# A planned attention, MoE and soft-MoE kernel on one core: new planner costs, w_in scaled by column block, a fourth scale part, the last g on VectorE, Exp loaded behind the last Mish

## The chip, the cores and the metric

The kernel runs on one core of one Trainium2 chip. The metric is device time in microseconds: the median of several executions, and lower is better. The engines are named as the profile names them: PE is TensorE (PEld its weight loads), ACT is ScalarE, DVE is VectorE, POOL is GpSimd, and SP issues the transfers.

## The reference

Three layers follow each other. The first is attention with a causal window of 64 keys, over 4 batches, 8 heads, 576 positions and head size 64. Its output is a matrix x of 2304 tokens by 512. The second is a dense layer pair with the Mish function between. The third is a soft mixture of experts with 32 slots.

```python
x = softmax(mask(q @ k.T / 8)) @ v              # per head; then 2304 x 512
h = x @ w_in                                    # 512 -> 2048
g = h * tanh(softplus(h))                       # Mish
x = g @ w_out                                   # 2048 -> 512
logits = x @ phi                                # 512 -> 32 slots
d = softmax(logits, axis=0);  slot_in = d.T @ x
slot_out[e] = relu(slot_in[e] @ w1[e]) @ w2[e]  # 8 experts, 4 slots each
out = softmax(logits, axis=1) @ slot_out
```

## The kernel before

The 2304 tokens are cut into 18 tiles of 128. **Attention** of a tile t has these operations, named by their planner names: qk (scores s, PE), max and neg (DVE), exp (ACT), sum and rcp (DVE), nrm (normalisation of p, POOL), tr (transposes pt on PE), tre (copies pts, ACT), pv (px on PE) and x (copy of the result). **The first dense layer** splits x and w_in into a high and a low half-precision part (xh and xl; wh and wl), so that each 128x512 block of h takes 12 matmuls; the planner cuts them into two halves, mm{t}_{m}a and mm{t}_{m}b, for the four column blocks m = 0 to 3 of w_in. ACT applies Mish (mi), and g is split again into gh and gl (gg in the profile). **w_out is never multiplied token by token**: the weights of w_out and phi are joined first (wpmm; wt are the tiles of the transposed w_out), so logits (lg) come from g directly, and the sum over tokens d.T @ g is kept up to date block by block of one or two tiles (bm, bexp, A, Aup). g is transposed by DMA (gT), for the last tile by PE (pghT, pglT). **The tail** multiplies that sum with w_out (si), then runs the experts: w1 (eh) and w2 (eo, by column blocks W2C), and last the outputs (fo, ob, out).

Weights arrive as 64-bit numbers and are decoded: a load of 512 KB (wir, wtr, wor), one ACT operation (wiy, wty, woy; L274) and two on DVE (L279, L283). Expert weights w are loaded as they are: 64 loads of 512 KB.

What sets the order of the work: a planner (class Plan) that runs when the program is built. Each operation has an engine, a cost in microseconds, a due time, operations that it depends on, and buffers that it takes and gives back (49 slabs of SBUF, 8 banks of PSUM, and counts that limit a kind). The planner steps through time; whenever an engine is free it issues the ready operation with the lowest due time whose buffers are free. Costs and due times are numbers in the dictionary PRM and in the calls of op. SAME and INTO are delays that it adds between operations. The result is a fixed order for each engine, and the same order for the DMA issues on SP's queue.

When PE has nothing to do in three stretches (from the start to qk0, from there to mm0_3a, and from the last h to t1_0), the planner issues a filler matmul there, 128x256 (fill, L194; pad in the profile). Fillers are instructions like others: once in the order, PE runs them whether it would have waited or not.

ACT holds one function table at a time. Exp and the decoding operation share one ("E"), Mish has the other ("M"), and copies run with either. Where the order changes from one to the other, an ACT_TABLE_LOAD stands between.

Scales: x and v are scaled by powers of two that come from running maxima of v over parts of the tiles (PART: three parts, tiles 0 to 3, 4 to 9 and 10 to 17). The chain that makes a scale is scale_ops (tr, mx, bc, f1 to f4).

Of the kernel before, what the change touches and what calls it, by code (L numbers as in the profile page):

```python
# [8 lines left out]
F32 = mybir.dt.float32  # L9
# [25 lines left out]
class Plan:  # L35


    SAME = {"DVE": 0.13, "ACT": 0.09, "PE": 0.0, "POOL": 0.0, "SP": 0.0, "NONE": 0.0}
    INTO = {"DVE": 0.2, "ACT": 0.2, "PE": 0.16, "POOL": 0.2, "SP": 0.1, "NONE": 0.0}
    DMA = 2.2  # L40
    SWITCH = 1.3
# [39 lines left out]
    def give(self, o):  # L81
        for key in o[7]:
            self.refs[key] -= 1
            if not self.refs[key]:
                p, i = self.where[key]
                q = p.rstrip("!^")
                self.free[q].append(i)
                if p != q:
                    self.held[p] -= 1

    def emit(self):
# [16 lines left out]
        while events:  # L108
# [6 lines left out]
            for eng in list(ready):  # L115
# [44 lines left out]
def body(tc, a):  # L160
# [7 lines left out]
    with ctx:  # L168
# [38 lines left out]
        sc = fix.tile([128, 56], F32, name="sc")  # L207
# [3 lines left out]
        SX, IX, SP_, IP, IL, C30, C31, CP, WM, SW, IW, INVH, GW, GV, GP_, RAT = 0, 3, 6, 7, 8, 11, 14, 17, 20, 24, 28, 32, 44, 48, 51, 52  # L211
        PART = [0 if t < 4 else 1 if t < 10 else 2 for t in range(NT)]
# [46 lines left out]
        def decode_ops(nm, src, n, where, dst, t_ld, t_dec, ld_deps, dst_get, y_eng):  # L259
# [25 lines left out]
            for j in range(n):  # L285
# [132 lines left out]
        for t in range(NT):  # L418
# [3 lines left out]
            for c in [1, 0] if 2 * t % 9 == 8 else [1]:  # L422
                one, end = t in (0, 4, 10) and c == 1, t in (3, 9, 17)
# [5 lines left out]
            for h in range(2):  # L429
                e = k + 2.6 * h  # L430
                op(f"max{t}_{h}", "DVE", 0.7, e + 1.5, lambda t=t, h=h: t_max(t, h), [f"qk{t}"] + ([f"max{t}_0"] if h else []))
                op(f"neg{t}_{h}", "DVE", 0.1, e + 1.5, lambda t=t, h=h: t_neg(t, h), [f"max{t}_{h}"])
                op(f"exp{t}_{h}", "ACT", 2.35 if t < P["SUMA"] else 1.5, e + 2, lambda t=t, h=h: t_exp(t, h), [f"neg{t}_{h}"] + ([f"exp{t}_0"] if h else []),
                   get=[] if h else [(f"p{t}", "s!"), (f"P{t}", "pp")], rel=[f"s{t}_{h}", f"S{t}_{h}"], table="E")
                if t >= P["SUMA"]:
                    op(f"sum{t}_{h}", "DVE", 0.7, e + 3, lambda t=t, h=h: t_sum(t, h), [f"exp{t}_{h}"] + (["sum%d_0" % t] if h else []))
                if h:
                    op(f"rcp{t}", "DVE", 0.25, e + 4, lambda t=t: t_rcp(t), [f"sum{t}_1" if t >= P["SUMA"] else f"exp{t}_1"])
                op(f"nrm{t}_{h}", *(("POOL", 1.3) if t < P["NRM"] else ("DVE", 0.72)), e + 4.5, lambda t=t, h=h: t_norm(t, h), [f"rcp{t}"] + ([f"nrm{t}_0"] if h else []))
                op(f"tr{t}_{h}a", "PE", 0.55, e + 5.5, lambda t=t, h=h: a_tr(t, h), [f"nrm{t}_{h}", "cst"], get=[(f"pt{t}_{h}", "b")], rel=[f"p{t}", f"P{t}"])  # L440
                op(f"tre{t}_{h}", "ACT", 0.62, e + 5, lambda t=t, h=h: t_trev(t, h), [f"tr{t}_{h}a"] + ([f"tre{t}_0"] if h else []),
# [3 lines left out]
            op(f"x{t}", *(("ACT", 0.62) if t < P["XA"] else ("DVE", 0.7)), k + 9, lambda t=t: t_x(t), [f"pv{t}"] + ([f"x{t - 1}"] if t % 2 else []),  # L445
# [4 lines left out]
        decode_ops("wi", a["w_in"], 16, lambda j: (j % 4, j // 4), stg, lambda j: P["W0"] + P["W_SP"] * j,  # L450
                   lambda j: P["W_DEC"] * (j + 1), [], "s", "POOL")
# [51 lines left out]
        for i, t in enumerate((3, 9, 17)):  # L503
# [56 lines left out]
        op("wpev", "DVE", 0.6, tw, wphi_ev, ["wpmm3"], get=[("wps", "s")], rel=["wpo"])  # L560
# [3 lines left out]
        for i in range(3):  # L564
            op(f"wpil{i}", "DVE", 0.15, tw if i == 0 else ta((3, 9, 17)[i]) - P["LEAD"] + 10, lambda i=i: wphi_il(i), ["p_f3", f"invc{i}"])
        op("wph", "ACT", 0.6, tw, wphi_h, ["p_s", "wptr"])
# [66 lines left out]
        for t in range(NT):  # L633
            t0 = T2 + TT * t
            last = [f"x{t // 2}"]
            op(f"xh{t}", "DVE", 0.54, t0 - 5, lambda t=t: x_h(t), [f"v{PART[t]}_s", f"x{t}"] + ([f"xh{t - 1}"] if t else []), get=[] if t % 2 else [(f"xx{t // 2}", "s!"), (f"XX{t // 2}", "x2")], rel=last)
            op(f"xl{t}", "DVE", 0.8, t0 - 4, lambda t=t: x_l(t), [f"xh{t}"], rel=last)
            for m in range(4):
# [5 lines left out]
                op(f"mi{t}_{m}", "ACT", 0.69, k + 2.7, lambda t=t, m=m: u_mish(t, m), [f"invh{PART[t]}_{0 if PART[t] else m}", f"mm{t}_{m}b"] + ([f"mi{t}_{m - 1}"] if m % 2 else []),  # L644
                   get=[] if m % 2 else [(f"u{t}_{h}", "s!"), (f"U{t}_{h}", "u")], rel=[f"h{t}_{m}"], table="M")
            U = units(t)
            for i, (h, c, n) in enumerate(U):
# [31 lines left out]
        op("idh", "DVE", 0.1, 60, id_half, ["cst"])  # L679

# [100 lines left out]
        for b in range(NBLK):  # L781
# [10 lines left out]
            op(f"lr{b}", "DVE", 0.3 + 0.07 * n, e, lambda b=b: b_lr(b), [f"lg{b}_{n - 1}_1", f"wpil{PART[t]}"], rel=[f"lg{b}"])  # L792
# [401 lines left out]
```

## Time and profile before

| what | value |
|---|---|
| median of 3 runs | 397.94 us (397.88 to 398.8) |
| profiled execution: time | 398.63 us |
| its span, first to last instruction | 396.8 us |
| mean granted clock of TensorE in the span | 0.986 |
| PE, ACT, DVE, POOL busy | 97%, 69%, 68%, 24% |
| moved by DMA | 102.67 MB, 259 GB/s |

The span is 1.8 us below the profiled execution's time, and that execution is 0.7 us above the median. The stages by the clock of the trace: the first scores at 6.4 us, the first block of h at 46.3 us, the last px at 224.5 us, the last block of h ends at 324.6 us, the experts begin at 344 us, the span ends at 396.8 us.

### The profile page before, as it was taken

What the parts mean: (1) busy time and instruction counts of PE and PEld (TensorE: products, weight loads), DVE (VectorE), ACT (ScalarE), POOL (GpSimd) and SP (SyncE); (2) the same over time, 40 slices, a digit from 0 to 9 for tenths busy, and PEclk for the clock granted to TensorE, in tenths of its full rate; (3) what the DMA queues carried; (4) which work ended last, traced back from release to release, by engine and by line L of the source; (5) the groups of instructions that cost most, each with busy time, mean ns of one, the idle gap of its engine ahead of it and who ended that gap; (6) DMA issues with size and microseconds to landing.
All of it is one profiled execution on the core that took longest, in us unless ns stands there. A gap on an engine that the chain in (4) does not pass through costs nothing.

```text
span 396.8 us, 10326 instructions
## 1 busy us (share of the span) xinstructions
PE 383.6 (97%) x4245; PEld 227.2 (57%) x4245; DVE 268.6 (68%) x579; ACT 275.8 (69%) x461; POOL 97.2 (24%) x82
## 2 busy tenths in 40 slices
PE   8999999999999999999999999999999999998982
PEld 6887758555465565566455644444454457636552
DVE  1799888879998969669899977455343374342342
ACT  1677799799986899878898399999655653102131
POOL 0243420205762222247140412121211240100000
PEclk9999999999999999999999999999999999999986
DMA  7999997131599784368999899999998889699997
GB/s 266 403 411 405 393 378 266 59 123 40 101 233 279 276 283 161 116 157 213 219 162 217 173 275 252 292 283 261 265 220 244 244 247 367 249 412 408 405 358 232
DMA packets 100686, 102.67 MB, mean 259 GB/s; under 512 B 74016, under 2 KB 81312, under 8 KB 100640
## 3 DMA queue, kind: packets, MB, share of 16 engines
q1 hardware_dynamic: 100640, 102.02, 85.9%
q8 instruction: 33, 0.54, 0.5%
q14 instruction: 13, 0.11, 0.1%
HBM read 79.46 MB, written 4.72 MB: 212 GB/s over the span
## 4 chain that ended last, share of the span: by engine, by line
PE 89%; DMA 4%; DVE 3%; issue 2%; ACT 0%; SPq 0%; DVEq 0%
PE h L587 47%; PE pad L194 6%; PE px L398 5%; PE pt L385 4%; PE eo L924 4%; PE eh L892 3%; PE s L332 3%; PE A L766 3%; DMA v<-in_vL 3%; PE lg L690 2%; PE lg L692 2%; PE fo L977 1%; DMA q<-in_qL 1%; PE gram_v L374 1%; PE s L323 1%
## 5 line engine op out<-in xcount | busy, mean ns | idle before, releaser
L587 PE MATMUL h<-wh,xx 128*128 128x512 f16 x576 | 184.3, 379 | 0.0
L587 PEld LDWEIGHTS <-xx 128*128 128x128 f16 x864 | 80.4, 98 | 86.4 <-issue 1.8
L587 PE MATMUL h<-wl,xx 128*128 128x512 f16 x288 | 109.1, 379 | 0.0
L364 POOL TENSOR_TENSOR p<-p,st 128x512 f32<-128x512 f32 x36 | 45.7, 1289 | 121.9 <-DVE st L344 34.1
L607 POOL TENSOR_SCALAR gg<-u,sc 128x1024 f16<-128x1024 f32 (+1 forms) x38 | 47.7, 1261 | 108.8 <-ACT u L593 86.1
L593 ACT ACTIVATE u<-h,sc 128x512 f32<-128x512 f32 x72 | 48.4, 686 | 28.0 <-PE h L587 23.4
L612 DVE SCALAR_TENSOR_TENSOR gg<-u,sc,gg 128x1024 f16<-128x1024 f32 (+1 forms) x38 | 50.3, 1332 | 13.8 <-POOL gg L607 13.8
L593 ACT ACT_TABLE_LOAD x41 | 52.6, 1283 | 2.0 <-PE h L587 1.3
L350 ACT ACTIVATE p<-s,st 128x128 f32<-128x128 f32 x144 | 41.8, 377 | 2.8 <-DVE st L344 2.5
L194 PE MATMUL pad<-wphi 128*64 128x256 f16 x259 | 36.5, 290 | 0.9 <-DVE wphi L204 0.9
L194 PEld LDWEIGHTS <-wphi 128*64 128x64 f16 x259 | 27.7, 116 | 5.5 <-issue 2.1
L390 ACT COPY pts<-pt 128x512 f32<-128x512 f32 x36 | 20.9, 588 | 11.4 <-PE pt L385 8.3
L341 DVE TENSOR_REDUCE st<-s 128x4 f32<-128x512 f32 x36 | 24.6, 683 | 5.4 <-PE s L332 5.4
L274 ACT ACT_TABLE_LOAD x19 | 24.4, 1283 | 1.0 <-PEq L1187 0.7
L356 DVE TENSOR_REDUCE st<-p 128x4 f32<-128x512 f32 x34 | 22.9, 674 | 2.4 <-ACT p L350 2.4
L385 PE MATMUL pt<-cst,p 128*128 128x128 f32 x144 | 21.6, 278 | 0.0
L398 PE MATMUL px<-pts,v 128*64 128x64 f32 x576 | 21.4, 225 | 0.0
L398 PEld LDWEIGHTS px<-pts,v 128*64 128x64 f32 x576 | 18.9, 138 | 3.7 <-issue 3.1
L332 PE MATMUL s<-k,q 64*64 64x128 f32 x576 | 18.8, 269 | 0.4 <-DMA q<-in_qL 0.4
L385 PEld LDWEIGHTS pt<-cst,p 128*128 128x128 f32 x144 | 16.1, 141 | 5.3 <-issue 3.0
L332 PEld LDWEIGHTS s<-k,q 64*64 64x64 f32 x576 | 16.9, 133 | 1.9 <-issue 0.7
L924 PE MATMUL eo<-w,hT 128*32 128x128 f32 (+1 forms) x384 | 16.9, 317 | 1.0 <-issue 1.0
(175 smaller groups left out, 491.8 us busy)
## 6 DMA issues: line engine op xcount, KB each, us to landing
w<-in_wL SPq DMA_DIRECT2D x64, 512.0 KB, 6.6
v<-in_vL SPq DMA_DIRECT2D x18, 512.0 KB, 8.3
wir<-in_w_in SPq DMA_DIRECT2D x16, 512.0 KB, 9.7
wtr<-in_w_outT SPq DMA_DIRECT2D x16, 512.0 KB, 4.9
wor<-in_w_out SPq DMA_DIRECT2D x16, 512.0 KB, 5.2
k<-in_kL SPq DMA_DIRECT2D x12, 512.0 KB, 8.8
q<-in_qL SPq DMA_DIRECT2D x9, 512.0 KB, 10.2
out<-ob SPq DMA_DIRECT2D x17, 256.0 KB, 3.9
```

The lines of the kernel that those rows point to most:

```text
L194: PE.matmul(pad, lhsT=hot, rhs=hot.unsqueeze(1).to_broadcast([128, 4, 64]), start=True, stop=True)
L332: PE.matmul(st_[t][h][64 * c:64 * c + 64, p], lhsT=qt[t // 2][r, t % 2, p, 64 * c:64 * c + 64], rhs=kt[g // 3][r, p, 64 * (g % 3):64 * (g ...
L341: DVE.tensor_reduce(stat[t][:, 0, 4 * h:4 * h + 4], st_[t][h], AX.X, ALU.max)
L350: ACT.activation(pr[t][:, h, p], st_[t][h][:, p], AF.Exp, scale=0.125, bias=stat[t][:, 0, 4 * h + p:4 * h + p + 1], accum_out=(stat[t][:, ...
L364: (POOL if t < P["NRM"] else DVE).tensor_tensor(pr[t][:, h], pr[t][:, h], r, ALU.mult)
L385: PE.transpose(q[:, p], pr[t][:, h, p], ident)
L398: PE.matmul(x[64 * h:64 * h + 64, p, f], lhsT=vt[t][:, c, 64 * (2 * p + h):64 * (2 * p + h) + 64], rhs=ptS[t][:, h, p, f], start=True, sto ...
L587: PE.matmul(ph[t, m], lhsT=xh[t][:, l, kk], rhs=r[m][:, kk], start=(kk == 0 and i == 0), stop=(kk == 3 and i == 2))
L593: ACT.activation(ub[t, h][:, m % 2], ph[t, m], AF.Mish, scale=col(INVH + 4 * PART[t] + m))
L607: POOL.tensor_scalar(o, u, col(CP + PART[t]), 1.0, ALU.mult, ALU.mult)
L612: DVE.scalar_tensor_tensor(gg[t, h][:, 1, c:c + n], flat(ub[t, h], c, n), col(CP + PART[t]), gg[t, h][:, 0, c:c + n], ALU.mult, ALU.subtract,)
L924: PE.matmul(tl["o", c][32 * j:32 * j + 32], lhsT=tl[f"hT{i}"][:, 128 * (kf + k) + 32 * j:128 * (kf + k) + 32 * j + 32], rhs=v[:, j, k], st ...
```

## The change

The planner's rules change in three ways. First, the costs of most operations are replaced, nearly always by smaller ones, and the delay between engines is now PIPE of the first engine plus INTO of the second. Second, a method latest gives all operations that follow the h blocks of tiles 16 and 17 a new due time, counted back along their longest chain of users from one end time XE. Third, all numbers of PRM are new; w_in's four column blocks have due times of their own (WM for loads, DM for decoding, WSM for scaling), and SP's first four loads are those of block 0. Besides: the parts of the scale are four (tiles 0 and 1, 2 and 3, 4 to 7, 8 to 17); gh of tiles 5 to 17 is made by DVE and no longer by POOL; the normalisation of tiles 16 and 17 and three of the eight halves of wh go to DVE, x of ten tiles to ACT; blocks of two tiles reach to tile 15; w2's columns are cut as 256, 128, 64 and 64 (before 128, 256 and 128); and an Exp of one element (wexp) follows the last Mish.

```diff
 PRM = dict(
-    FOP=70.175, SUMA=1, XA=3, WHA=8, KEEP=7, MOSTA=0, ...
+    WM=(-49.02, 2.55, 20.34, 26.82), DM=(-22.13, 7.04, 25.37, 45.14), WSM=(-7.03, 15.22, 40.15, 75.45), PB=(2, 4,
+    8), LT=16, XE=405.787, FOP=-76.351, SUMA=4, XA=10, WHA=5, KEEP=30, MOSTA=1, ...
...
-    SAME = {"DVE": 0.13, "ACT": 0.09, "PE": 0.0, "POOL": 0.0, "SP": 0.0, "NONE": 0.0}
-    INTO = {"DVE": 0.2, "ACT": 0.2, "PE": 0.16, "POOL": 0.2, "SP": 0.1, "NONE": 0.0}
+    SAME = {"DVE": 0.13, "ACT": 0.14, "PE": 0.0, "POOL": 0.1, "SP": 0.0, "NONE": 0.0}
+    INTO = {"DVE": 0.13, "ACT": 0.13, "PE": 0.1, "POOL": 0.13, "SP": 0.1, "NONE": 0.0}
+    PIPE = {"DVE": 0.09, "ACT": 0.1, "PE": 0.16, "POOL": 0.06, "SP": 0.0, "NONE": 0.0}
...
+    def latest(self, first, end):
...
+            way[i] = o[2] + (self.DMA if o[1] == "SP" else 0.0) + max(
+                (way[u] + (self.SAME[o[1]] if self.ops[u][1] == o[1] else self.PIPE[o[1]] + self.INTO[self.ops[u][1]]) for u in users[i]), default=0.0)
...
+            self.ops[i] = o[:3] + (end - way[i],) + o[4:]
...
-        PART = [0 if t < 4 else 1 if t < 10 else 2 for t in range(NT)]
+        PB = P["PB"]
+        PART = [sum(t >= b for b in PB) for t in range(NT)]
...
-                op(f"exp{t}_{h}", "ACT", 2.35 if t < P["SUMA"] else 1.5, ...
+                op(f"exp{t}_{h}", "ACT", 1.37 if t < P["SUMA"] else 1.0, ...
...
-                e = "POOL" if t < P["FAST"] else "DVE"
+                e = "POOL" if t < min(P["FAST"], P["PET"]) else "DVE"
...
+        def warm_exp():
+            tl["wx"] = wk.tile([1, 1], F32, tag="wx", name="wx", bufs=1)
+            ACT.activation(tl["wx"], ident[0:1, 0:1], AF.Exp)
+
+        op("wexp", "ACT", 0.2, 0.0, warm_exp, [f"mi{NT - 1}_3"], table="E")
...
-            op(f"sT{i}", "POOL", 0.9, f, lambda i=i: tail_zero(f"sT{i}"), [f"mm{NT - 1}_3b"], get=[(f"sT{i}", "s^")])
+            op(f"sT{i}", "POOL", 0.9, f, lambda i=i: tail_zero(f"sT{i}"), [f"mm{NT - 1}_0b"], get=[(f"sT{i}", "s^")])
...
+        plan.latest([f"mm{t}_0a" for t in range(P["LT"], NT)], P["XE"])
         plan.emit()
```

How the order moves, at three places. The first is SP's queue at the start of the program, before:

```order
L298 DMA cb_70<-in_masks 128x384
L308 DMA k0_86<-in_kL 128x1024
L312 DMA q0_94<-in_qL 128x1024
L266 DMA wir0_102<-in_w_in 128x1024
L299 DMA cst_69<-in_cst 128x128
L266 DMA wir1_112<-in_w_in 128x1024
L308 DMA k1_140<-in_kL 128x1024
```

and with the change:

```order
L300 DMA wir0_81<-in_w_in 128x1024
L300 DMA wir1_92<-in_w_in 128x1024
L300 DMA wir2_100<-in_w_in 128x1024
L300 DMA wir3_110<-in_w_in 128x1024
L332 DMA cb_70<-in_masks 128x384
L342 DMA k0_122<-in_kL 128x1024
L346 DMA q0_136<-in_qL 128x1024
```

The first q moves from the second 512 KB load to the sixth, behind the whole first column block of w_in.

The second is ACT's queue in the middle of attention (p<-s are four Exp, pts<-pt copies, wty decoding, u<-h Mish; the number behind a name is the tile's), before:

```order
L593 ACT_TABLE_LOAD
L593 ACTIVATE u4_0_1808<-h4_0_1488,sc_74 128x512
L593 ACTIVATE u4_1_1837<-h4_2_1748,sc_74 128x512
L593 ACTIVATE u4_0_1808<-h4_1_1682,sc_74 128x512
L350 ACT_TABLE_LOAD
L350 ACTIVATE p11_1864<-s11_0_1812,st11_1848 128x128 x4
L390 COPY pts10_1897<-pt10_0_1871 128x512
L350 ACTIVATE p11_1864<-s11_1_1813,st11_1848 128x128 x4
```

and with the change:

```order
L627 ACT_TABLE_LOAD
L627 ACTIVATE u3_1_1458<-h3_3_1715,sc_74 128x512
L424 COPY pts11_1850<-pt11_1_1852 128x512
L384 ACT_TABLE_LOAD
L384 ACTIVATE p13_1902<-s13_0_1790,st13_1848 128x128 x4
L384 ACTIVATE p14_1943<-s14_0_1859,st14_1900 128x128 x4
L424 COPY pts12_1959<-pt12_0_1948 128x512
L384 ACTIVATE p13_1902<-s13_1_1791,st13_1848 128x128 x4
```

Before, the Mish of tile 4 stands between the Exp of tiles 10 and 11. With the change only tile 3 is through Mish when tile 13 is at its Exp: attention is pulled ahead, and u4 to u17 come mostly behind it. ACT_TABLE_LOAD falls from 83 to 67 in the whole program, and from 48 to 28 up to the last pts.

The third is ACT's queue at the last Mish, before:

```order
L593 ACTIVATE u17_1_4501<-h17_3_4493,sc_74 128x512
L630 COPY gT17_0_4529<-pghT17_1_4522 128x512
L630 COPY gT17_0_4529<-pglT17_0_4531 128x512
L630 COPY gT17_1_4567<-pglT17_2_4571 128x512
L630 COPY gT17_1_4567<-pghT17_3_4606 128x512
L731 ACT_TABLE_LOAD
L731 ACTIVATE e49_4599,bst9_4618<-lt9_4603,mrun1_76 128x128
```

and with the change:

```order
L627 ACTIVATE u17_1_4407<-h17_3_4409,sc_74 128x512
L718 ACT_TABLE_LOAD
L718 ACTIVATE wx_4490<-cst_69 1x1
L664 COPY gT17_1_4503<-pglT17_2_4493 128x512
L664 COPY gT17_1_4503<-pghT17_3_4505 128x512
L772 ACTIVATE e48_4536,bst8_4520<-lt8_4498,mrun0_75 128x128
```

The table load moves from right ahead of the first Exp of the tail to ahead of the last two copies. On PE the fillers fall from 259 to 153: 44 ahead of the first scores (before 25), 53 from there to the h blocks of tile 0 (before 166), 56 in the tail (before 68). All other matmuls stay, but for w2's 64-wide blocks (128 of 64 columns in place of 64 of 128).

## Rows read from the trace of the kernel before

**Rows 1.** The page's first part: busy us, share, instructions.

```profile
PE 383.6 (97%) x4245; PEld 227.2 (57%) x4245; DVE 268.6 (68%) x579; ACT 275.8 (69%) x461; POOL 97.2 (24%) x82
```

**Rows 2.** Busy time by stage.

```profile
core 0: us, PE busy (x) PEld busy (x) DVE busy (x) ACT busy (x) POOL busy (x), PEclk, DMA share, GB/s
...
46.30:100.00 53.70, 53.70 (x518) 32.16 (x515) 46.35 (x110) 48.57 (x73) 12.79 (x10) 1.00 0.50 185
100.00:178.00 78.00, 78.00 (x874) 45.10 (x872) 64.73 (x127) 66.64 (x125) 28.59 (x22) 1.00 0.72 204
178.00:224.50 46.50, 45.45 (x562) 26.82 (x560) 43.73 (x85) 38.06 (x58) 19.53 (x15) 1.00 1.04 205
224.50:324.60 100.10, 100.10 (x804) 48.55 (x805) 53.27 (x102) 75.85 (x93) 19.98 (x19) 1.00 0.99 250
```

**Rows 3.** Groups by line: the fillers.

```profile
L194 PE MATMUL pad<-wphi 128*64 128x256 f16 x259 | 36.5, 290 | 0.9 <-DVE wphi L204 0.9
```

**Rows 4.** PE's timeline from the start: start us, us, instruction.

```profile
0.95 5.54 PE L194 MATMUL pad<-wphi 128*64 128x256 f16 x25 [0.95 <-DVE wphi L204]
...
7.30 1.10 PE L332 MATMUL s<-k,q 64*64 64x128 f32 x32 [0.39 <-DMA q<-in_qL]
8.34 4.77 PE L194 MATMUL pad<-wphi 128*64 128x256 f16 x42
```

**Rows 5.** ACT's timeline from the start.

```profile
8.76 0.67 ACT L274 ACTIVATE wiy<-wir 128x512 f32<-128x512 f32 x1 [6.75 <-DMA wir<-in_w_in]
...
20.75 1.07 ACT L390 COPY pts<-pt 128x512 f32<-128x512 f32 x2 [0.36 <-PE pt L385]
```

**Rows 6.** The chain that ended last, in order of time, first pieces.

```profile
7.18 9.96 DMA v<-in_vL
```

**Rows 7.** ACT's timeline from 180 us.

```profile
180.49 1.14 ACT L350 ACTIVATE p<-s,st 128x128 f32<-128x128 f32 x4
181.50 0.69 ACT L274 ACTIVATE woy<-wor 128x512 f32<-128x512 f32 x1
182.07 0.60 ACT L390 COPY pts<-pt 128x512 f32<-128x512 f32 x1
...
185.20 1.28 ACT L593 ACT_TABLE_LOAD   x1
186.50 1.26 ACT L593 ACTIVATE u<-h,sc 128x512 f32<-128x512 f32 x2
```

**Rows 8.** Busy time in slices of 25 us, columns as in group 2.

```profile
75.00:100.00 25.00, 25.00 (x224) 13.71 (x223) 21.75 (x51) 23.04 (x32) 7.29 (x6) 1.00 0.19 65
...
250.00:275.00 25.00, 25.00 (x192) 12.18 (x191) 13.00 (x24) 24.64 (x29) 4.47 (x4) 1.00 1.08 285
```

**Rows 9.** PE's timeline behind the last h.

```profile
328.84 0.40 PE L625 MATMUL pglT<-idh,gg 128*128 128x128 f16 x4
...
336.33 0.83 PE L766 MATMUL A<-gg,e 128*32 128x512 f16 x12
```

**Rows 10.** DVE's timeline there.

```profile
327.05 0.75 DVE L612 SCALAR_TENSOR_TENSOR gg<-u,sc,gg 128x512 f16<-128x512 f32 x1
...
335.23 0.18 DVE L753 SCALAR_TENSOR_TENSOR e<-et,e 128x32 f16<-128x32 f32 x1
```

**Rows 11.** POOL's timeline there.

```profile
325.60 0.69 POOL L607 TENSOR_SCALAR gg<-u,sc 128x512 f16<-128x512 f32 x1
```

**Rows 12.** SP's queue: the last run of weight loads.

```profile
321.78 49.94 SPq L831 DMA_DIRECT2D w<-in_wL  x39
```

**Rows 13.** Busy time around the loads of group 12, columns as in group 2.

```profile
320.00:345.00 25.00, 25.00 (x286) 16.64 (x283) 11.93 (x35) 7.51 (x17) 5.21 (x8) 1.00 0.82 277
345.00:380.00 35.00, 32.32 (x478) 17.11 (x478) 12.60 (x34) 6.11 (x12) 0.90 (x2) 0.98 1.02 406
```

**Rows 14.** PE's timeline near the end.

```profile
383.54 0.64 PE L924 MATMUL eo<-w,hT 128*32 128x128 f32 x16
...
389.06 2.10 PE L977 MATMUL fo<-so,cT 128*128 128x128 f16 x18 [1.36 <-DVE so L962]
```

More of the change, by code (lines that the diff above doesn't have):

```diff
@@ L89, in give @@
                     self.held[p] -= 1
+    def latest(self, first, end):
+        n = len(self.ops)
+        users = [[] for _ in range(n)]
+        for i, o in enumerate(self.ops):
+            for d in o[5]:
+                users[self.index[d]].append(i)
+        way, todo = [0.0] * n, [len(u) for u in users]
+        stack = [i for i in range(n) if not todo[i]]
+        while stack:
+            i = stack.pop()
+            o = self.ops[i]
+            way[i] = o[2] + (self.DMA if o[1] == "SP" else 0.0) + max(
+                (way[u] + (self.SAME[o[1]] if self.ops[u][1] == o[1] else self.PIPE[o[1]] + self.INTO[self.ops[u][1]]) for u in users[i]), default=0.0)
+            for d in o[5]:
+                d = self.index[d]
+                todo[d] -= 1
+                if not todo[d]:
+                    stack.append(d)
+        stack, seen = [self.index[x] for x in first], set()
+        while stack:
+            i = stack.pop()
+            if i in seen or self.ops[i][1] == "SP":
+                continue
+            seen.add(i)
+            stack += users[i]
+        for i in seen:
+            o = self.ops[i]
+            self.ops[i] = o[:3] + (end - way[i],) + o[4:]
     def emit(self):
@@ L422, in body @@
             for c in [1, 0] if 2 * t % 9 == 8 else [1]:
-                one, end = t in (0, 4, 10) and c == 1, t in (3, 9, 17)
+                one, end = t in (0, *PB) and c == 1, t in ENDS
                 op(f"vg{t}_{c}", "PE", 0.29, k - P["LEAD"] + 6, lambda a_=(t, c, one, end): v_gram(*a_), [f"v{t}"] + ([] if one and c else [f"vg{t}_1" if not c else f"vg{t - 1}_{int((2 * t - 2) % 9 != 8)}"]),
@@ L444, in body @@
                rel=[f"pts{t}", f"PT{t}", f"v{t}", f"V{t}"])
[L445 removed]
+            op(f"x{t}", *(("ACT", 0.48) if t < P["XA"] else ("DVE", 0.61)), k + 9, lambda t=t: t_x(t), [f"pv{t}"] + ([f"x{t - 1}"] if t % 2 else []),
                get=[] if t % 2 else [(f"x{t // 2}", "s!")], rel=[f"px{t}"])
         stg, wh, wl = {}, {}, {}
[L450 to L451 removed]
+        decode_ops("wi", a["w_in"], 16, lambda j: (j % 4, j // 4), stg, lambda j: P["WM"][j // 4] + P["W_SP"] * (j % 4),
+                   lambda j: P["DM"][j // 4] + P["W_DEC"] * (j % 4), [], "s", "POOL")
         def win_all(m):
@@ L563, in body @@
         scale_ops("p", lambda: col(GP_), "wpmx", tw, SP_, IP, False)
-        for i in range(3):
-            op(f"wpil{i}", "DVE", 0.15, tw if i == 0 else ta((3, 9, 17)[i]) - P["LEAD"] + 10, lambda i=i: wphi_il(i), ["p_f3", f"invc{i}"])
-        op("wph", "ACT", 0.6, tw, wphi_h, ["p_s", "wptr"])
+        for i in range(len(ENDS)):
+            op(f"wpil{i}", "DVE", 0.15, tw if i == 0 else ta(ENDS[i]) - P["LEAD"] + 10, lambda i=i: wphi_il(i), ["p_f3", f"invc{i}"])
+        op("wph", "ACT", 0.5, tw, wphi_h, ["p_s", "wptr"])
         op("wpl", "DVE", 1.05, tw, wphi_l, ["wph"], rel=["wpt"])
@@ L840, in tail_zf @@
         def tail_zf():
[L841 removed]
+            DVE.tensor_scalar(tl["z"][:, 2:3], tl["z"][:, 1:2], col(C30 + len(PB)), 8.0, ALU.mult, ALU.mult)
         def tail_at():
@@ L1098, in body @@
             for i in range(2):
-                op(f"thT{h}{i}", "ACT" if i else "DVE", 0.35, f, lambda h=h, i=i: tail_hT(h, i), [f"tho{h}", f"hT{i}"], rel=[f"ho{h}"])
+                op(f"thT{h}{i}", "ACT" if i else "DVE", 0.27, f, lambda h=h, i=i: tail_hT(h, i), [f"tho{h}", f"hT{i}"], rel=[f"ho{h}"])
         def tail_ones():
```

85 lines of the change are left out of this document (43 added, 42 removed).

## The prediction

> **What bounds the kernel now.** I read the page first, then the busy time by stage, then PE's timeline where it has gaps, last the other engines where PE may wait for them. The page has PE at 97% and no other engine over 69% [rows 1]. By stage PE is never idle from 46.3 to 178 us nor from 224.5 to 324.6, and idle for 1.05 us between [rows 2]. The reader should not take this as useful work throughout: 259 fillers stand in it, 36.5 us busy [rows 3], and PE runs each in its turn. So up to 324.6 us the kernel is what PE was given: useful matmuls and fillers. ACT idles 11.4 us of the 78 from 100 to 178, and 24.3 of the 100.1 behind 224.5 [rows 2]: there it waits for PE, not PE for it. Behind 324.6 the program is a chain of small steps and then the experts.
>
> **What that makes of the change.** The useful matmuls stay, so the place where the last h ends moves by what is added or removed in front of them: fillers, the start, and any new idle time. I count against 324.6 us and then the tail.
>
> Fillers between the first scores and h of tile 0: 166 before, 53 with the change. A run of 42 starts at 8.34 and lasts 4.77 us, the last one's 0.27 us included; the spacing is 0.11 us [rows 4]. 113 times 0.11 is 12.4 us less. That is a saving only where PE has something ready in place of them; what is not ready comes back below as idle time.
>
> The start: scores of tile 0 need the first q. Before, q was the second 512 KB load and the scores began at 7.30 [rows 4]. The third such load ends ACT's wait at 8.76 [rows 5], and the ninth, v of tile 0, lands at 7.18 + 9.96 = 17.14 [rows 6]: six loads in 8.4 us, 1.4 each. With the change q is the sixth load, so 8.76 + 3 x 1.4 = 12.9 us; the scores begin 5.6 us later. The 44 fillers ahead cost nothing: 25 took 5.54 us at 0.22 each [rows 4], so 44 end by 10.6 us at the latest, before q is there. The two sums over the first w_in blocks, 1.2 us, now run in that wait (less 1.2). One more scale chain puts two small matmuls on PE, 0.4 us. In all -12.4 + 5.6 - 1.2 + 0.4 = -7.6 us.
>
> **New idle time** is the unknown. Up to the last px attention now takes nearly all of ACT: by the order, 28 table loads, 32 decodings, 36 groups of four Exp, 46 copies, 21 Mish and 5 wh stand up to the last pts copy. Prices: load and start of the next operation 1.30 us (185.20 to 186.50), Exp group 1.01 (180.49 to 181.50), decoding 0.57 (181.50 to 182.07), Mish 0.58 (two in 1.26, the last one's end included) [rows 7], copy 0.48 (two in 1.07) [rows 5], wh twice a Mish, as it is twice as wide. Sum: 36 + 18 + 36 + 22 + 12 + 6 = 130 us, of which 11 stand ahead of the first pts copy. Before, 48 loads stood there, 26 us more. That copy was 13.4 us behind the first scores (20.75 less 7.30) [rows 4, 5]; with Exp held up by two wh I take 24 us for it, an estimate. So ACT needs 119 us from 24. If it is filled as from 75 to 100 us, 92%, it ends at 153.5; as from 250 to 275 us, 99%, at 144.5 [rows 8]; as from 100 to 178 us, 85% [rows 2], at 163.5. The last px is 1.5 us behind. PE's own count for it: behind the last px come 101 halves of h, all the logits and eight updates of A, some 161 us at the spacings of before; with the last h at 324.6 - 7.6 = 317, minus 161, that is 156. The pieces ahead of it, summed from the start, give 152 instead, since small gaps between matmuls fall somewhere; I use 154. So at 92% PE waits about 1 us, at 99% not at all, at 85% 11 us. I take 3 us: the first, and some 2 for waits that fall inside the stretch though the sums balance (DVE's scale chains, v of tile 2, which is the twentieth load and lands at 8.76 + 17 x 1.4 = 32.6 us where PE, by the sum of its pieces, wants it near 30). Bounds: 0 and 11.
>
> Here a rule of the Trainium skill speaks against any order that depends on ACT. The row has a load of 1.28 us and the next operation 1.30 after the load's start [rows 7]. The page ScalarE: Activation LUTs, section What ACT_TABLE_LOAD costs, states 1283 ns and a drain of about 1380 ns on top, 2.66 us a switch. By the page 28 loads would take 38 us more and attention would end some 38 us later; the trace shows no drain behind a load, so the sum goes by the row.
>
> Edits at nothing, each with its cover: gh of 13 tiles on DVE is about 18 us (24 wide and 4 half ones at some 0.7 and 0.4, estimated from ACT's 0.58 for half the width), behind the last px; DVE is busy 53.3 of 100.1 us there [rows 2], so it fits, and without that cover the next h would wait for PSUM by the same 18 us at most. The 16 fewer loads, 21 us of ACT, are worth nothing behind the last px, where ACT has 24 us free; ahead of it they are in the sum above. Loads on SP: the first column block delays k and v by the 5.6 us already counted.
>
> **The tail** is 72.2 us now (324.6 to 396.8). The last gh runs on POOL from 325.60 for 0.69, its gl on DVE begins only at 327.05 [rows 10, 11]; both on DVE, gl should start near 325.9: up to 1.1 less, I take 0.8. PE's fillers overrun what they wait for: the transposes of that gl start at 328.84, 1.04 behind its end, and the last A at 336.33, 0.92 behind its operand [rows 9, 10]. 12 fillers fewer (1.3 us) take some of that: 1.3. The early Exp load takes 1.3 us off the first Exp of the tail, but that is not what the last A waits for: 0 (bound 1.3). At the end, eight weight tiles are cut in 64 columns instead of 128: twice the matmuls. A tile takes 0.57 us at 128 (16 records in 0.64, the last one's end included) [rows 14]; 32 records at the 27 ns of the scores (32 in 0.87, by the 1.10 of rows 4 less one record's length) give 0.86. Eight times 0.29 is 2.3 us more; cost by columns alone would be 0. The last block's 18 output matmuls take 2.10 us [rows 14] and would halve, with shorter scaling around them: 1.5 less. I take +0.8 for both. Tail: -0.8 - 1.3 + 0.8 = -1.3 us, bounds -4 and +2.
>
> Transfers do not take that back: 39 loads stood behind the last transpose, issued over 49.9 us [rows 12]; now 41, 2 x 1.3 = 2.6 more; but DMA was idle for 18% of 320 to 345 us [rows 13], 4.5 us, since loads waited for slabs.
>
> **Sum:** -7.6 + 3 - 1.3 = -5.9 us. Against the profiled execution that is a span of 390.9 and a time of 392.7; against the median, 0.7 us lower, 392.0 us.
>
> **Rivals.**
> *Attention starves PE (slower).* Fillers and too high costs made the old order loose, so that every operand was there in time. An order with exact costs has no such cover. Its place is ACT's queue from 24 us to the last pts: filled only to 85%, as from 100 to 178 us, it costs 11 us of idle PE where I counted 3, and the time is 400.0. Against it: ACT idled there because PE was full, and reached 99% elsewhere [rows 2, 8]. No gain is left once idle time is 8.9 us, that is once ACT is filled to less than 87%. With w2's 64-wide blocks at their bound it is 402.
>
> *The gain is eaten.* ACT at 86 to 87%, or transfers that come 3 us late at the tail, where DMA is at 1.02 from 345 to 380 [rows 13]: 396.8 to 399.
>
> *Nothing lost.* No idle time and the tail at -4: -7.6 - 4 = -11.6, 386.3 us. For it: the fillers' places show that the planner now sees PE ready there. Against it: five engines in fixed orders rarely meet without waits.
>
> **How the numbers follow.** This kernel's runs tell apart about 0.3%, 1.2 us. My forecast, 388 to 396.7, has 0.55; nothing lost, 386 to 388, 0.14; eaten, 0.11; starved, 0.20. Faster 0.69, same 0.11, slower 0.20. The range 386 to 402 leaves out a little of the last and of the second; the forecast's own range is 388 to 396.7.
>
> **What would show it.** Right: PE's first scores at 12 to 13.5 us; the last px at 152 to 158; the last h ending at 318 to 322; 153 fillers; the tail 69 to 73 us; 67 table loads of 1.28. Wrong: PE idle over 9 us between 46 us and the last h, with ACT's Exp or copies as releasers; eo waiting for w loads; a granted clock under 1 before 360 us, which gaps in a stretch without fillers could bring.

## The result: 0.9% slower, and VectorE sets the pace of attention

The changed kernel takes 401.6 us (median of 4 runs, 400.59 to 402.3) against 397.91 for the kernel before: a ratio of 1.0088, 95% interval 1.006 to 1.0117. The profiled execution took 402.3 us with a span of 400.3.

The page of the changed kernel, first part and the chain by engine (before: [rows 1]):

```profile
PE 373.7 (93%) x4300; PEld 217.2 (54%) x4300; DVE 281.1 (70%) x612; ACT 255.4 (64%) x473; POOL 55.9 (14%) x50
...
PE 55%; DVE 21%; DMA 19%; issue 2%; ACT 1%; SPq 0%; ACTq 0%
```

PE is 10 us less busy, as fillers left, and yet the span is 3.5 us longer: PE waits now. The reader should see that VectorE's share of the whole span, 70%, tells nothing of a bound. The busy time by stage does (columns as in [rows 2]):

```profile
6.40:31.50 25.10, 23.94 (x367) 18.16 (x365) 20.45 (x53) 17.95 (x66) 6.36 (x6) 1.00 1.03 409
31.50:75.00 43.50, 42.16 (x469) 26.60 (x465) 41.41 (x117) 39.88 (x81) 11.46 (x11) 1.00 0.83 320
75.00:150.00 75.00, 66.39 (x901) 42.33 (x902) 74.58 (x135) 68.67 (x147) 31.88 (x25) 1.00 0.72 198
150.00:175.00 25.00, 24.34 (x293) 14.32 (x291) 18.73 (x54) 16.13 (x24) 2.24 (x2) 1.00 0.59 143
175.00:325.00 150.00, 148.35 (x1222) 72.25 (x1223) 92.25 (x168) 92.08 (x120) 1.90 (x2) 1.00 0.92 212
```

From 75 to 150 us VectorE is busy for 74.58 of 75 us, ScalarE for 68.67, and PE idles 8.6 us. Most of PE's idle time there ends when POOL has normalised p, and POOL's normalisation in turn waits longest in total for VectorE's reciprocals (us in total, times, longest):

```profile
POOL p L398 <- DVE st L394: 14.2, 3, 5.8
...
PE pt L419 <- POOL p L398: 7.2, 9, 1.4
```

In the kernel before, VectorE had 64.73 of the 78 us from 100 to 178 [rows 2].

PE's timeline of the changed kernel at the start, at the last px, and at the last A:

```profile
11.67 1.10 PE L366 MATMUL s<-k,q 64*64 64x128 f32 x32
...
31.54 0.39 PE L621 MATMUL h<-wh,xx 128*128 128x512 f16 x1
...
163.77 1.15 PE L432 MATMUL px<-pts,v 128*64 128x64 f32 x32
...
329.92 0.38 PE L621 MATMUL h<-wh,xx 128*128 128x512 f16 x1
...
339.40 0.83 PE L807 MATMUL A<-gg,e 128*32 128x512 f16 x12
```

The scores begin 4.4 us later (7.30 before, [rows 4]); the first h 14.7 us sooner and the last px 60.7 us sooner (46.3 and 224.5 us before); and still the last matmul of h starts 5.5 us later, at 329.92. Before it was:

```profile
324.40 0.38 PE L587 MATMUL h<-wh,xx 128*128 128x512 f16 x1
```

From there to the end of the span it is 70.4 us instead of 72.4: 2.0 less. That makes the 3.5. DMA's 19% of the chain are mostly loads up to 57.7 us; what a quicker start would be worth was not tested.

### The profile page after: what moved, and what is told of

It is laid out like the page before. It is cut to its first block, busy times and chain, and to the rows that moved or that the text cites. A ratio compares the mean times of both kernels' runs of the same rounds, so it can differ in the third digit from the quotient of the medians.

```text
span 400.3 us, 10431 instructions
## 1 busy us (share of the span) xinstructions
PE 373.7 (93%) x4300; PEld 217.2 (54%) x4300; DVE 281.1 (70%) x612; ACT 255.4 (64%) x473; POOL 55.9 (14%) x50
## 4 chain that ended last, share of the span: by engine, by line
PE 55%; DVE 21%; DMA 19%; issue 2%; ACT 1%; SPq 0%; ACTq 0%
PE h L621 31%; DMA wir<-in_w_in 6%; DMA k<-in_kL 5%; DMA gT<-gg 4%; PE eh L933 3%; PE eo L965 3%; DVE st L390 3%; DVE st L375 3%; PE A L807 3%; DVE gg L646 3%; PE lg L731 2%; DMA wtr<-in_w_outT 2%; DVE wt L317 2%; PE pad L226 2%; PE lg L733 2%
## 5 line engine op out<-in xcount | busy, mean ns | idle before, releaser
L384 ACT ACTIVATE p<-s,st 128x128 f32<-128x128 f32 x144 | 43.6, 391 | 10.4 <-DVE st L378 9.0
L398 POOL TENSOR_TENSOR p<-p,st 128x512 f32<-128x512 f32 x32 | 39.3, 1247 | 75.9 <-DVE st L394 43.0
L646 DVE SCALAR_TENSOR_TENSOR gg<-u,sc,gg 128x1024 f16<-128x1024 f32 (+1 forms) x38 | 49.0, 1291 | 0.6
L643 DVE TENSOR_SCALAR gg<-u,sc 128x1024 f16<-128x1024 f32 (+1 forms) x28 | 19.9, 711 | 26.8 <-ACT u L627 26.7
L419 PE MATMUL pt<-cst,p 128*128 128x128 f32 x144 | 22.5, 281 | 7.5 <-POOL p L398 7.5
L226 PE MATMUL pad<-wphi 128*64 128x256 f16 x153 | 23.3, 302 | 1.0 <-DVE wphi L236 1.0
L921 POOL MEMSET sT<- 128x1024 f32 x2 | 1.9, 952 | 152.7 <-DVE gg L646 152.7
L226 PEld LDWEIGHTS <-wphi 128*64 128x64 f16 x153 | 17.1, 122 | 4.8 <-issue 2.1
L390 DVE TENSOR_REDUCE st<-p 128x4 f32<-128x512 f32 x28 | 18.6, 672 | 0.4 <-ACT p L384 0.4
```

The source lines that it names most:

```text
L226: PE.matmul(pad, lhsT=hot, rhs=hot.unsqueeze(1).to_broadcast([128, 4, 64]), start=True, stop=True)
L384: ACT.activation(pr[t][:, h, p], st_[t][h][:, p], AF.Exp, scale=0.125, bias=stat[t][:, 0, 4 * h + p:4 * h + p + 1], accum_out=(stat[t][:, ...
L390: DVE.tensor_reduce(stat[t][:, 1, 4 * h:4 * h + 4], pr[t][:, h], AX.X, ALU.add)
L398: (POOL if t < P["NRM"] else DVE).tensor_tensor(pr[t][:, h], pr[t][:, h], r, ALU.mult)
L419: PE.transpose(q[:, p], pr[t][:, h, p], ident)
L646: DVE.scalar_tensor_tensor(gg[t, h][:, 1, c:c + n], flat(ub[t, h], c, n), col(CP + PART[t]), gg[t, h][:, 0, c:c + n], ALU.mult, ALU.subtract,)
```

## The experiments

Theory: VectorE bounds attention in the new order, in part because its instructions take longer than their own length while POOL works. Rivals: ScalarE bounds it, as the prediction's rival said; the fillers still set PE's end; the way from Exp to the transposes is too long. All kernels keep the order of the one they are made from, and only what an operation issues is edited.

### Whose work is on the path: dve_plus, act_plus, dve_minus

dve_plus does ten row sums of p twice, act_plus ten copies of pts, and dve_minus reads 32 of the 128 columns in 28 row sums, which leaves out part of the sum.

```diff
-            DVE.tensor_reduce(stat[t][:, 1, 4 * h:4 * h + 4], pr[t][:, h], AX.X, ALU.add)
+            for _ in range(2 if t >= 8 and h else 1):
+                DVE.tensor_reduce(stat[t][:, 1, 4 * h:4 * h + 4], pr[t][:, h], AX.X, ALU.add)
```

```diff
-            ACT.copy(ptS[t][:, h], pt_[t, h])
+            for _ in range(2 if t >= 8 and h else 1):
+                ACT.copy(ptS[t][:, h], pt_[t, h])
```

```diff
-            DVE.tensor_reduce(stat[t][:, 1, 4 * h:4 * h + 4], pr[t][:, h], AX.X, ALU.add)
+            DVE.tensor_reduce(stat[t][:, 1, 4 * h:4 * h + 4], pr[t][:, h, :, 48:80], AX.X, ALU.add)
```

> The changed kernel in its own order, with the second row sum of p of tiles 8 to 17 made twice on DVE: ten more reductions of 0.6 us, in the stretch in which DVE is busy 74.6 of 75 us (75 to 150). Theory 1, DVE bounds the attention stretch: the last px moves from 163.8 to about 169 and the time rises by 5 to 6 us, to 407. Rival, ACT bounds it, as the prediction had it: DVE has room, the time stays within 1 us of 401.6. Rival, loads by DMA set it: within 1 us too.

> The changed kernel in its own order, with the second copy of pts of tiles 8 to 17 made twice on ACT: ten more copies of 0.47 us in the stretch from 75 to 150, where ACT is busy 68.7 of 75 us. Theory 1, DVE bounds the stretch: part of the 4.7 us goes into ACT's idle time, 0 to 2 us more, up to 403.5. Rival, ACT bounds it: 4 to 5 us more, about 406. Rival, loads: within 1 us.

> The changed kernel in its own order, with the row sums of p on DVE over 32 of the 128 keys (this leaves out part of the softmax's sum): 28 reductions of 0.2 instead of 0.6 us, 11 us less of DVE up to the last px. Theory 1, DVE bounds: the last px comes 6 to 10 us earlier (other engines are close behind), the time falls to 392 to 396, under the kernel before. Rival, ACT bounds: within 1.5 us of 401.6. Rival, loads: within 1 us.

Measured: dve_plus 410.1 us, ratio to the kernel before 1.0282 (1.0243 to 1.0322); act_plus 402.87, 1.0115 (1.0089 to 1.014); dve_minus 396.93, 0.996 (0.9936 to 0.9985). Against the changed kernel's 1.0088 that is +7.7 us for ten more row sums on VectorE, +1.1 for ten more copies on ScalarE, and -5.1 for the shorter row sums. In the whole program VectorE's busy time went from 281.1 us to 289.7 in dve_plus (8.6 more, as a row sum takes 0.68 us and other instructions got longer) and to 270.4 in dve_minus (10.7 less). The last matmul of px starts at 173.6, 167.5 and 159.7 us (changed kernel 164.7). I had expected 407 us and some 5 us at the last px for dve_plus, and at most 396 us and 6 to 10 us for dve_minus: both missed, dve_plus costs more and dve_minus gains less. The stretch from 75 to 150 us by busy time (columns as in [rows 2]) in dve_plus:

```profile
75.00:150.00 75.00, 62.56 (x846) 39.70 (x845) 74.42 (x126) 62.65 (x129) 30.26 (x24) 0.98 0.65 184
```

in act_plus:

```profile
75.00:150.00 75.00, 66.53 (x901) 42.66 (x899) 74.65 (x131) 70.82 (x151) 33.16 (x26) 1.00 0.69 198
```

and in dve_minus:

```profile
75.00:150.00 75.00, 71.16 (x953) 45.42 (x952) 72.11 (x148) 72.78 (x154) 30.15 (x24) 1.00 0.69 198
```

VectorE stays full in the first two, and in this stretch PE loses only where VectorE has more to do. So the rivals that ScalarE or the loads set the pace alone fall: both allowed dve_plus 1 us at most. ScalarE is close behind, though: of its 4.7 us 2.8 show at the last px. In the third it is at 97% and looks like the next bound, and less than half of what VectorE was given came out.

### Why VectorE is full: pool_small and pool_scratch

The lines of VectorE from 40 to 155 us in the changed kernel (count, then busy us and mean ns of one):

```profile
L375 DVE TENSOR_REDUCE st<-s 128x4 f32<-128x512 f32 x26 | 17.4, 674 | 0.0
L646 DVE SCALAR_TENSOR_TENSOR gg<-u,sc,gg 128x1024 f16<-128x1024 f32 x8 | 12.7, 1593 | 0.0
L313 DVE TENSOR_SCALAR wt<-wty 128x512 uint32<-128x512 uint32 x15 | 9.9, 659 | 0.0
L378 DVE TENSOR_SCALAR st<-st 128x4 f32<-128x4 f32 x26 | 8.5, 327 | 0.0
L503 DVE SCALAR_TENSOR_TENSOR wl<-wi,sc,wh 128x1024 f16<-128x1024 f32 x6 | 8.4, 1404 | 0.0
```

327 ns is odd for 4 columns (neg, L378). Single ones show it, in VectorE's timeline:

```profile
105.22 0.16 DVE L393 TENSOR_SCALAR st<-st 128x8 f32<-128x8 f32 x1
...
107.02 1.00 DVE L378 TENSOR_SCALAR st<-st 128x4 f32<-128x4 f32 x1
107.93 0.68 DVE L375 TENSOR_REDUCE st<-s 128x4 f32<-128x512 f32 x1
108.54 1.10 DVE L317 SCALAR_TENSOR_TENSOR wt<-wtr,wt 128x512 uint32<-128x512 uint32 x1
109.56 0.16 DVE L378 TENSOR_SCALAR st<-st 128x4 f32<-128x4 f32 x1
```

and in POOL's:

```profile
105.75 2.24 POOL L398 TENSOR_TENSOR p<-p,st 128x512 f32<-128x512 f32 x2 [5.79 <-DVE st L394]
107.98 1.12 POOL L641 TENSOR_SCALAR gg<-u,sc 128x1024 f16<-128x1024 f32 x1
```

A neg begun at 107.02, inside POOL's normalisation, ends with it at about 107.98 and takes 1.00 us; one at 109.56, when POOL is done, takes 0.16. The reduction from 107.93 runs beside POOL's gh at its usual 0.68, and the decoding step from 108.54 is 0.4 longer than without POOL. The stretching is not new: in the kernel before, neg has a mean of 305 ns over the same time. What is new is that VectorE has no time to spare. pool_small cuts POOL's normalisation to 16 of 128 columns; pool_scratch does the same and then gives POOL its work back on a buffer whose content nobody uses.

```diff
+            if t < P["NRM"]:
+                POOL.tensor_tensor(pr[t][:, h, :, 56:72], pr[t][:, h, :, 56:72], r[:, :, 56:72], ALU.mult)
+                POOL.tensor_tensor(junk, pr[t][:, h], r, ALU.mult)      # pool_scratch alone
+                return
```

> The changed kernel, its order kept, with POOL's normalisation of p cut from 128 to 16 of the 128 key columns (the rest of p stays unnormalised: that part of the softmax is left out). VectorE's instructions and their number stay. Theory 'VectorE bounds attention, and POOL's instructions stretch VectorE's': neg falls from 327 ns to about 200, wtb from 644 to near 520, VectorE's busy time from 75 to 150 us falls below 73 of 75 us, the last px comes 3 to 6 us before 163.8, and the time is 396 to 399. Rival 'VectorE's durations do not depend on POOL': neg, wtb and gl keep their means within 5%, the last px stays within 1.5 us of 163.8 (the chain max, exp, sum, nrm, tr is only shorter), and the time is 400 to 402.5.

> As pool_small (POOL normalises 16 of 128 key columns, so that part of the softmax is left out), but behind each of these 32 small operations POOL multiplies the whole 128x512 block of p into a buffer that nobody reads. POOL is as busy as in the changed kernel; the way from Exp to the transposes is as short as in pool_small. Theory 'POOL's instructions stretch VectorE's': neg is back above 300 ns (pool_small 196), wtb above 600 (447), gl above 1540 (1369), the last px starts within 3 us of 163.8, and the time is 398.5 to 402.5. Rival 'the gain of pool_small was the shorter way from Exp to the transposes': the last px stays within 2 us of pool_small's 154.5 and the time is 391.5 to 394.

Measured: pool_small 392.24 us, 0.9862 (0.9823 to 0.9901); pool_scratch 402.92, 1.0117 (1.009 to 1.0143). The last matmul of px starts at 155.5 and 166.7 us (changed kernel 164.7). The same lines of pool_small:

```profile
L375 DVE TENSOR_REDUCE st<-s 128x4 f32<-128x512 f32 x26 | 17.5, 677 | 0.0
...
L650 DVE SCALAR_TENSOR_TENSOR gg<-u,sc,gg 128x1024 f16<-128x1024 f32 x8 | 10.9, 1369 | 0.0
L507 DVE SCALAR_TENSOR_TENSOR wl<-wi,sc,wh 128x1024 f16<-128x1024 f32 x6 | 7.7, 1281 | 0.0
L313 DVE TENSOR_SCALAR wt<-wty 128x512 uint32<-128x512 uint32 x16 | 7.1, 447 | 0.0
...
L378 DVE TENSOR_SCALAR st<-st 128x4 f32<-128x4 f32 x26 | 5.1, 196 | 0.0
```

and of pool_scratch:

```profile
L376 DVE TENSOR_REDUCE st<-s 128x4 f32<-128x512 f32 x26 | 17.5, 675 | 0.0
L318 DVE SCALAR_TENSOR_TENSOR wt<-wtr,wt 128x512 uint32<-128x512 uint32 x14 | 12.9, 929 | 0.0
L651 DVE SCALAR_TENSOR_TENSOR gg<-u,sc,gg 128x1024 f16<-128x1024 f32 x8 | 11.6, 1456 | 0.0
L508 DVE SCALAR_TENSOR_TENSOR wl<-wi,sc,wh 128x1024 f16<-128x1024 f32 x6 | 9.2, 1534 | 0.0
L314 DVE TENSOR_SCALAR wt<-wty 128x512 uint32<-128x512 uint32 x14 | 8.7, 623 | 0.0
L379 DVE TENSOR_SCALAR st<-st 128x4 f32<-128x4 f32 x26 | 7.0, 270 | 0.0
```

The stretch from 75 to 150 us (columns as in [rows 2]) in pool_small, then in pool_scratch:

```profile
75.00:150.00 75.00, 72.65 (x998) 47.06 (x1000) 72.08 (x155) 74.25 (x152) 16.16 (x25) 1.00 0.73 206
...
75.00:150.00 75.00, 65.24 (x890) 41.60 (x888) 74.65 (x127) 66.18 (x142) 40.09 (x43) 1.00 0.68 198
```

With POOL busy for half as long as in the changed kernel (16.16 us of the 75 against 31.88), gl, wl, the first decoding step and neg get 9 to 40% shorter, and the reductions stay at 674 to 677 ns. With the work given back to POOL, and some more (40.09 us), they are longer again and the whole gain is gone. In the whole program the 612 instructions of VectorE were busy for 281.1 us in the changed kernel, 264.9 in pool_small and 282.3 in pool_scratch. The expectations missed in size: pool_small gained 9.4 us where I had 3 to 6, and in pool_scratch neg (above 300) and gl (above 1540) stayed lower, as the stretching fell on other lines (the second decoding step at 929).

The rival of the shorter way from Exp to the transposes is not closed by pool_scratch alone. Each tile is normalised in two halves, and there only the first half's way is as short as in pool_small. The second half stands behind the first one's full multiplication: both are done 1.8 us after the first began (from 106.61 us), in pool_small 0.5 (from 99.65), in the changed kernel 2.2 (from 105.75). PE waits for POOL's p for 8.0 us from 75 to 150, in the changed kernel for 7.2, in pool_small not at all. But 5.6 of the 8.0 us end with first halves. And VectorE has little time free in the changed kernel: 0.42 us of the 75, and 5.4 us in all from 31.5 us to the last px (busy for 126.95 of 132.3). A shorter way alone can't bring px 9 us sooner while VectorE still needs the same time for its work. So the gain comes at least in part, and by these numbers mainly, from VectorE's shorter instructions; a smaller share of the shorter way is not ruled out.

Four lines alone (gl, wl, L313, neg), count times difference of the means of the changed kernel and pool_small, give 1.8 + 0.7 + 3.2 + 3.4 = 9.1 us; the last px came 9.2 us sooner. That the two agree is chance, since VectorE was spared 16.2 us in the whole program.

The Trainium skill, page SBUF — State Buffer, section Who interferes with whom, states this as a rule: one pair of SBUF ports is shared by VectorE and GpSimd; where a VectorE instruction in a mode of two ports meets GpSimd, the first to come holds the pair for its whole instruction, and the other blocks; reductions on this chip never take it. The trace agrees in both points (1.00 us against 0.16; 674 to 677 ns throughout), though no view shows the mode of an instruction.

The planner knows of this overlap, in both kernels, but limits what it can cost:

```python
                if eng == "DVE" and o[0].startswith(self.SBUF):
                    both = max(0.0, busy.get("POOL", 0.0) - t)
                    cost += min(cost * 0.72, both * 0.42)
```

An operation can grow by 0.72 of its own cost at most. neg, with a cost of 0.07 us in the changed kernel, becomes 0.12 at most; the trace has a mean of 0.33 and single ones of 1.00. POOL's normalisation costs 1.07 in the planner and 1.31 in the trace from 40 to 155 us. No run changed these numbers.

### The same saving in both orders: after_eps, before_eps

18 VectorE operations that add 1e-9 to sums of at least 1 are left out, of the changed kernel and of the one before.

```diff
-            DVE.tensor_scalar(stat[t][:, 1], stat[t][:, 1], 1e-9, None, ALU.add)
```

> The changed kernel, its order kept, without the 18 VectorE operations that add 1e-9 to the sums of p (189 ns each, 3.4 us in all; each sum is at least 1, where adding 1e-9 changes no bit). Theory 'VectorE bounds attention': each microsecond off VectorE is worth some 0.5 to 1.3 (dve_minus 0.45, dve_plus 1.3), so the last px starts 1.5 to 4.4 us sooner and the time is 397 to 399.8. Rival 'VectorE is one of several, and small savings vanish': within 0.8 us of the changed kernel, 400.6 to 402.2.

> The same 18 operations left out of the kernel before. Theory 'PE with its fillers sets the pace there, VectorE does not': within 0.3% of before, the last px within 0.5 us of 224.4. Rival 'VectorE bounds both orders': 1.5 to 4 us less.

Measured: after_eps 399.69 us, 1.0034 (1.0016 to 1.0052), some 2.1 below the changed kernel; before_eps 398.03, 0.9996 (0.998 to 1.0013). The last matmul of px starts at 162.2 instead of 164.7, and at 225.4 instead of 225.3. 3.4 us of VectorE are worth 2.1 in one order and nothing in the other.

### What the fillers were worth: after_nofill, before_nofill, nofill_all

fill() issues its matmul only in some of its three stretches (0: ahead of the first scores, 1: from there to h of tile 0, 2: the tail).

```diff
-            PE.matmul(pad, lhsT=hot, rhs=..., start=True, stop=True)
+            if k != 1:        # after_nofill, before_nofill;  nofill_all: if k == 0
+                PE.matmul(pad, lhsT=hot, rhs=..., start=True, stop=True)
```

> The changed kernel, its order kept, without its 53 fillers between the first scores and h of tile 0 (53 x 0.11 = 5.8 us of PE). Theory 'VectorE bounds attention': the fillers only filled waits, the first h comes at most 1 us sooner, the last px stays within 1.5 us of 163.8, and the time is 400 to 402.5. Rival 'PE's sum still sets the end': all is 5 to 6 us sooner, the time is 395.5 to 397.

> The kernel before in its own order, without the 166 fillers between the first scores and the h blocks of tile 0 (18.3 us of PE). If each filler stood where PE had work ready, as the prediction counted the 113 that the change takes out, the time falls by up to 18 us less the waits that then show. If the fillers stood where PE would have waited for DVE, ACT or loads anyway, the time stays within 1 us of 397.9. DVE is busy 23.0 of 25 us from 25 to 50 us and loads run at 400 GB/s to 60 us, so I expect 1 to 4 us less, 394 to 397.

> The kernel before without the 166 fillers behind the first scores and also without the 68 of the tail. The prediction had the tail's fillers overrun what they wait for (1.04 and 0.92 us at two places) and gave 1.3 us to 12 fewer. By that: 1.3 to 2.0 us less than without the 166 alone, a ratio to before of 0.984 to 0.987. Rival 'they cover waits, and without them the granted clock falls in the tail': no gain or up to 2 us more, 0.989 to 0.995.

Measured: after_nofill 401.06 us, 1.007 (1.0049 to 1.009), not told apart from the changed kernel; before_nofill 394.51, 0.9893 (0.9876 to 0.9909); nofill_all 391.67, 0.9831 (0.9804 to 0.9859). The start of before_nofill, by busy time:

```profile
6.40:46.30 39.90, 30.00 (x483) 23.59 (x484) 33.87 (x84) 28.82 (x81) 12.39 (x10) 0.83 1.03 401
```

and from the waits (in total, times, longest):

```profile
PE gram_v L375 <- DMA v<-in_vL: 4.9, 3, 4.1
PE s L333 <- DMA k<-in_kL: 2.9, 1, 2.9
PE pt L386 <- POOL p L365: 1.6, 2, 1.3
```

166 fillers at 0.11 us are 18.3 us of PE, and taking them out gave 4.3. The rest turned mostly into idle time of PE, 9.9 us in this stretch (0.6 before), which waits for v, k and the normalisation, and the granted clock of this stretch fell from 1.00 to 0.83, a mean of time at 2.4 and at 1.2 GHz, behind those waits. With the same fillers out it was 0.96 in nofill_all and 0.79 in nofill_tail. So most of the fillers stood where PE would have waited, and only those that overran a wait cost time. In the tail it is 68 fillers, 7.5 us at that spacing, for 2.5 us, a little more than the 2.0 at most that I had expected. The clock fell there too, in nofill_all:

```profile
325.00:345.00 20.00, 17.49 (x166) 7.32 (x162) 9.07 (x28) 3.17 (x11) 1.84 (x2) 0.74 0.82 315
```

The gain holds in spite of that. nofill_all is the fastest kernel of this study that computes all of it: 6.7 us below the one before.

### The tail: before_tail, nofill_tail

gh of tile 17 on VectorE and the early Exp, in the kernel before and in before_nofill:

```diff
             ACT.activation(ub[t, h][:, m % 2], ph[t, m], AF.Mish, scale=col(INVH + 4 * PART[t] + m))
+            if (t, m) == (NT - 1, 3):
+                ACT.activation(wk.tile([1, 1], F32, tag="wx", name="wx", bufs=1), ident[0:1, 0:1], AF.Exp)
...
-            if eng == "POOL":
+            if eng == "POOL" and t < NT - 1:
```

> The kernel before, its order kept, with two of the change's edits in the tail alone: gh of tile 17 on VectorE instead of POOL, and an Exp of one element right behind the last Mish. The prediction's terms: 0.8 us for gh, 0 for the Exp load, so 0.8 less than before, 397.1. Theory 'these two carry the 2.0 us by which the tail became shorter': 1.5 to 2.2 less, 395.8 to 396.5. Rival 'the tail shrank by its fillers, by the due times counted back from the end and by w2's blocks': within 0.4 us of before.

> The two edits of before_tail in the kernel before without its 166 fillers (which was 4.2 us faster than before). If the terms add: 4.2 plus what before_tail shows, 393 with the prediction's 0.8 and 392 with 2.0. Rival 'the tail's gain is taken back by the loads of the expert weights, which start no sooner': 394 to 394.8, as without the edits.

Measured: before_tail 399.11 us, 1.0025 (1.0007 to 1.0044); nofill_tail 395.19, 0.992 (0.9894 to 0.9947). Every expectation misses: together the two edits gain nothing in the old order, and before_tail is 1.0 us slower (nofill_tail is not told apart from before_nofill). ACT's timeline in before_tail behind the last Mish shows where:

```profile
325.24 0.69 ACT L593 ACTIVATE u<-h,sc 128x512 f32<-128x512 f32 x1 [1.90 <-PE h L587]
325.94 1.28 ACT L595 ACT_TABLE_LOAD   x1
327.24 0.20 ACT L595 ACTIVATE wx<-cst 1x1 f32<-1x1 f32 x1
327.35 0.56 ACT L632 COPY gT<-pghT 128x512 f16<-128x512 f16 x1
```

In this order three copies of gT that the logits wait for stand behind the last Mish, and the load and its Exp hold them up for 1.4 us. The last A starts 1.5 us later than before, 0.4 of which is there at the last h already. gh begins at 326.81 on VectorE, behind three copies of gT in its order, and not sooner than on POOL before (325.60, [rows 11]). In the changed kernel half of the transposes of tile 17 (16 of 32) and all but two of ACT's copies are done before the last h. So what made its tail 2.0 us shorter is probably this order with its due times counted back from the end, and not the two edits by themselves; that was read from the order and the traces, and no run made that part of the order alone.

## Why the prediction was wrong

**The failed step is the new idle time.** I counted 3 us: 1 from the sum of ScalarE's queue and some 2 for waits such as VectorE's scale chains. VectorE's own sum, 99% from 75 to 150 us in the new order, stands nowhere: its share of the span [rows 1] looked harmless. The rows had a warning: from 178 to 224.5 us, where attention ended and PE idled 1.05 us, VectorE was busy for 43.73 of 46.50 us, 94% [rows 2]. PE idles 13.4 us from 6.4 to 330.1 us (1.7 before, up to 324.6), so 11.8 were new: beyond the step's bound of 11. ScalarE was filled to 92% in the dense stretch, as reckoned, and yet that was not what PE waited for. Its sum was short as well: 125.2 us of work from 24 to 162 us where the step had 119; 3.4 of that are the accumulator reads behind the Exp of the first four tiles, which have no price there.

**The rival "attention starves PE"** gave the time within 2 us, 400.0, and the mechanism, an order without cover, but named the wrong queue: more work on ScalarE cost little (1.1 us for 4.7), more on VectorE nearly all of itself (7.7 for 8.6). Its 402 for w2's blocks at their bound does not follow, as the sum had their 2.3 us in it already.

**Fillers, start, sums.** Between the first scores and the last h PE's busy time fell from 315.84 to 305.75 us, 10.1 less. The steps had -12.4 for fillers, -1.2 for the sums of w_in and +0.4 for a scale chain; with some 0.9 for 16 transposes that moved ahead of the last h (0.45 for 8) that is -12.3, and 2.2 of it did not show, which I can't place. The scores came at 11.67, the step said 12.9. That fillers can be counted as a saving only where PE has work in their place was said in the prediction; before_nofill shows how seldom it has.

**Tail.** -1.3 predicted, -2.0 measured, within bounds, but partly by luck, as the parts were wrong. gh on VectorE and the early load brought nothing when put into the old order. The 64-wide blocks of w2 did not cost 2.3 us: a tile of 32 matmuls takes 0.58, about what 16 of twice the width did [rows 14], so cost goes by columns there. The last block's output matmuls fell from 2.10 to 0.69, by more than the half that the step gave; the granted clock was 0.50 at that place before (389.0 to 391.2 us) and is 1.00 now (391.7 to 392.5), so only a part of it is the width. From the changed kernel's PE timeline:

```profile
388.17 0.65 PE L965 MATMUL eo<-w,hT 128*32 128x64 f32 x32
...
391.74 0.69 PE L1018 MATMUL fo<-so,cT 128*128 128x64 f16 x18 [1.23 <-DVE so L1003]
```

From the last A to the end it is all the same 0.4 us longer than before. That the scale of w2's blocks is now worked out a fourth time may be the reason; no run tested it.

**Signs of the text.** 153 fillers and 67 table loads are there; the last px at 163.8 and the last h at 330 lie outside what the text had called right. PE idles for more than 9 us behind 46 us (11.7), a sign of being wrong in the text, but with VectorE's results and POOL's as releasers rather than ScalarE's.

## What to carry to other kernels

Before an order is made tighter, sum every engine's work over the stretch that gets denser, not over the span: here VectorE, ScalarE and PE all needed nearly the whole of it, and the one that nobody counted decided. What a planner adds for two engines that get in each other's way has to have the right form: here it grows with the length of VectorE's operation, while in the trace a small one beside a long one of POOL waits for its end. A filler costs only what it overruns, so test fillers by leaving them out: here that was worth 6.7 us in the old order, more than any gain of the new one.

## What was not expected of the hardware

POOL's 32 normalisations cost VectorE time though the two engines work on different data at that moment: cut to 16 of 128 columns, they left VectorE busy for 16.2 us less in the whole program, with the same 612 instructions. A 4-column operation took 1.00 us instead of 0.16. Leaving fillers out lowered the granted clock, at the start from 1.00 to 0.83 (0.96 and 0.79 in two other kernels without them) and in the tail to 0.74, and the kernel was faster all the same.
